# RWKV attention and two MLPs on one core: k transposes and y^T halves as single steps of the planner

## The chip, the cores and the metric

One NeuronCore of a Trainium2 chip. Its engines run side by side, each in its own program order: TensorE (PE) multiplies matrices, VectorE (DVE) and ScalarE (ACT) work element by element, GpSimd (POOL) and SyncE (SP) issue DMA transfers here. The metric is the device time of one execution in microseconds (us); before the change the median of three runs is 1027.59 us (1027.45 to 1028.16).

## The reference

An RWKV-like recurrence over 4 batches of 8 heads, 768 tokens and 48 dimensions per head, then a gated MLP (384 to 1536 to 384) and a second MLP with a leaky ReLU (384 to 2048 to 384) on 3072 tokens, all in float32:

```python
for t in range(S):
    kt, vt, rt, wt = (k[:, :, t], v[:, :, t], r[:, :, t], w[:, :, t])
    cur = np.einsum('bhd,bhe->bhde', u[None] * kt, vt)
    y[:, :, t] = np.einsum('bhd,bhde->bhe', rt, state + cur)
    state = wt[:, :, :, None] * state + np.einsum('bhd,bhe->bhde', kt, vt)
...
x = y.transpose(0, 2, 1, 3).reshape(B * S, H * D)
x = (x @ moe_w_a * (x @ moe_w_b)) @ moe_w_out
h = x @ moe2_w_in
out = (np.maximum(h, 0) + alpha * np.minimum(h, 0)) @ moe2_w_out
```

## The kernel before

**Units.** The recurrence is cut into 12 units: one unit is a chunk of 128 tokens of half of the (batch, head) pairs, so units 0 and 1 are the first chunk, 2 and 3 the second, and so on. A unit holds r, k and w transposed in tile T (112 partitions: two heads of 48 with a gap; 8 pairs; 128 tokens), and again in natural layout (128 tokens on the partitions) in tile N; v is in V. Its steps are:

- *natural* (DVE, lines 440 to 503): the C x C blocks on the diagonal of the chunk (C is 4 or 8 in units 0 to 3, 16 from unit 4 on), diagonal by diagonal: products for the decay (kn, N), a product into e and a reduction into A, of 16, 15, 14, ... columns a block. *diag* (SP, lines 505 to 522) sends A to DRAM (mb) and back into M with eight transfers.
- *tree* (DVE, lines 525 to 543): six steps h = 1, 2, 4, ... 32 on T, each a large one (1024 elements a partition) on r and k and a small one on w. *level* (PE, psl, lines 545 to 594): for each h from C on, the off-diagonal blocks of M by small matmuls from T, copied to M by ACT; level h needs the tree steps below h, so unit 3 (C = 8) begins with h = 8, behind the step h = 4.
- *ktrans* (lines 605 to 621): eight transposes of k on PE (psk), copied to kn by ACT in two groups of four.
- *dstate* (psd, lines 623 to 646): the chunk's contribution to the state; *state* (lines 651 to 693): copies of the state St to Z (ACT), its decay, and DVE's St += psd.
- *yout* (psx, lines 695 to 730): y^T from M and Z, two halves b of 64 matmuls each; each half goes to x as a rounded part (ACT) and a rest (DVE).

**MLP1** runs between the units on PE. A block j of 512 tokens (two units) takes 12 steps f: pa (nine matmuls, since float32 is split in two parts and three products of three matmuls are added), pb (nine), and acc for the step before (six, then three). Between them ACT copies pa to a, DVE multiplies a by pb (the product, `a<-a,pb`), ACT rounds it to g and DVE takes the rest (`g<-a,g`). Lines 257 (helper `tt`) and 769 (helper `mm`) show most of these instructions. Each block's MLP1 lies beside the next block's two units. Weights come in through POOL's DMAs and are unpacked by ACT and DVE (ws, w). **MLP2** (hp, acd) follows from about 613 us on, when all units are done.

**What sets the order.** `Tasks` (lines 35 to 208) is a list planner. Each step is added with an engine, a planned duration, a priority, the names that it reads and writes, and a pool from which it takes a buffer (`alloc`). `run` plays the plan forward: on each engine that is free it starts the ready step of lowest priority number, and emits the instructions in the order of planned starts. The hardware then keeps this order on every engine. A planned duration is thus no time on the chip, but it decides what the planner puts ahead of what. Pool psatt has three PSUM banks, given out in program order to psl, psk, psd, psx; psh has two (pa, pb, hp), so a pb takes the bank that the pb before it had, once DVE's product has read it; T, N, V, kn and e have one buffer each, so the next unit's T is loaded only when the tree, the levels and the transposes of this unit are done with T.

An empty PE step (duration 0, no instruction) can take a bank for a step that needs two; *dstate* did so already.

The calls of a unit that the change touches, priorities by `pr`:

```python
        for g in range(2):
            ktrans(g, pr(0.6))
        dstate(pr(0.65))
        ...
        yout(0, pr(0.8))
        yout(1, pr(0.85))
```

Of the kernel before, what the change touches and what calls it, by code (L numbers as in the profile page):

```python
# [7 lines left out]
F32 = mybir.dt.float32  # L8
# [26 lines left out]
class Tasks:  # L35
# [26 lines left out]
    def add(self, eng, dur, prio, fn, r=(), w=(), alloc=None, nbytes=0, work=0):  # L62


        i = len(self.t)
        deps = set()
        for x in r:
            if x in self.last_w:
                deps.add(self.last_w[x])
        for x in w:  # L70
            if x in self.last_w:
                deps.add(self.last_w[x])
            deps.update(self.readers.get(x, ()))
        for x in r:
            self.readers.setdefault(x, []).append(i)
        for x in w:
            self.last_w[x] = i
            self.readers[x] = []
        if alloc:
            tag, name = alloc  # L80
            self.handles[name] = (tag, [], i)
            self.pool_seq[tag].append(i)
        for x in list(r) + list(w):
            h = x.split("/")[0] if isinstance(x, str) else x
            if h in self.handles:
                self.handles[h][1].append(i)
                if self.handles[h][2] != i:
                    deps.add(self.handles[h][2])
        self.t.append([eng, dur, prio, fn, deps, alloc, nbytes])
        if work:  # L90
            self.work[i] = work
        return i
# [119 lines left out]
def rwkv_then_moe_kernel(  # L212
# [49 lines left out]
    def act(n, psum=False):  # L262
        return n / 1200 + (0.05 if psum else 0.093)
# [70 lines left out]
    X = {}  # L334

    def unit(u, pr):
# [265 lines left out]
            else:  # L602
                nc.scalar.copy(dst, src)

        def ktrans(g, p):
            st = {}
            ps = f"psk{u}_{g}"
            tag, pool = bank(False)

            def tr():  # L610
                st[g] = pp.tile([128, 4, 112], F32, tag=tag, name="psk", bufs=3)
                for i in range(4):
                    nc.tensor.transpose(st[g][:, i], cur["T", u][:, 1, 4 * g + i], idt[0:112, 0:112])

            def cp():
                if g == 0:
                    cur["kn", u] = new_kn().rearrange("p (q d) -> p q d", d=112)
                nc.scalar.copy(cur["kn", u][:, 4 * g:4 * g + 4], st[g])

            add("PE", 0.4, p, tr, r=[f"{T}/k.{g}", "idt"], w=[ps], alloc=(pool, ps), work=392)  # L620
            add("ACT", act(448, True), p, cp, r=[ps], w=[f"{kn}/{g}"], alloc=("kn", kn) if g == 0 else None)

        def dstate(p):

# [67 lines left out]

                add("ACT", act(384, True), p + 6, begin, r=[f"psd{u}_{cc}"], w=s)

        def yout(b, p):


            st = {}
            ps = f"psx{u}_{b}"
            t0 = 256 * (u - us[0]) + 128 * b  # L700
            tag, pool = bank(False)

            def mms():
                st["ps"] = pp.tile([128, 3, 128], F32, tag=tag, name="psx", bufs=3)
                for cc in range(2):
                    for q in range(4):
                        for s, c0, hd, beg, end in (
                                (2 * q, 0, 0, True, True), (2 * q + 1, 32, 1, True, True),
                                (8 + q, 32, 0, True, False), (8 + q, 0, 1, False, True)):
                            nc.tensor.matmul(  # L710
                                out=st["ps"][32 * (s % 4):32 * (s % 4) + 32, s // 4, 64 * cc:64 * cc + 64],
                                lhsT=zt(cc, hd)[:, 4 * b + q, c0:c0 + 32],
                                rhs=mt(hd)[:, cc, 4 * b + q],
                                start=beg, stop=end,
                            )

            def hi():
                if first:
                    X[j] = xp.tile([128, 2, 3, 256 * len(us)], F32R, tag="x", name="x", bufs=2)
                nc.scalar.copy(X[j][:, 0, :, t0:t0 + 128], st["ps"])  # L720

            def lo():
                tt(X[j][:, 1, :, t0:t0 + 128], st["ps"], X[j][:, 0, :, t0:t0 + 128].bitcast(F32), ALU.subtract)

            first = u == us[0] and b == 0
            add("PE", 1.56, p, mms, w=[ps], alloc=(pool, ps), work=2048,
                r=[mn(hd, k) for hd in range(2) for k in KM]
                + [zn(cc, hd, k) for cc in range(2) for hd in range(2) for k in "VS"])
            add("ACT", act(384, True), p, hi, r=[ps], w=[f"x{j}/{u}{b}h"], alloc=("x", f"x{j}") if first else None)
            add("DVE", dve(384), p, lo, r=[ps, f"x{j}/{u}{b}h"], w=[f"x{j}/{u}{b}l"])  # L730


        if u:
# [18 lines left out]
        for bs in parts_:  # L752
            for hd, b0 in ((0, 64), (1, 0)):
                e, d = ("DVE", dve(512 * len(bs), True)) if both and hd else ("ACT", act(512 * len(bs)))
                add(e, d, p, lambda hd=hd, b0=b0, bs=bs: rcopy(hd, b0, bs), r=nm(T + "/r", bs), w=[mn(hd, "R")])
        for g in range(2):
            ktrans(g, pr(0.6))
        dstate(pr(0.65))
        for cc in range(2):
            for bs in parts_:  # L760
                state(cc, bs, pr(0.7 + 0.05 * cc))
        yout(0, pr(0.8))
        yout(1, pr(0.85))

        return [f"x{j}/{u}{b}{z}" for b in range(2) for z in "hl"]

# [379 lines left out]
```

## Time and profile before

| | |
|---|---|
| median of 3 runs | 1027.59 us (1027.45 to 1028.16) |
| profiled execution | 1034.63 us, span 1032.8 us |
| mean granted PE clock | 0.986 |
| PE busy | 988.8 us (96%) |
| DVE busy | 728.4 us (71%) |
| ACT busy | 434.1 us (42%) |
| POOL busy | 95.7 us (9%) |
| chain that ended last | PE 65%, DVE 12%, ACT 10%, DMA 9%, issue 3%, SPq 1% |

Read the table by stretches. Up to some 83 us the first units run almost alone; from there to 541 us units and MLP1 share PE; from 613 us on it is MLP2. In a timeline row, the first number is the start, the second the duration, then come the engine, the line, the operation and the tiles (out <- in), shapes and the count of instructions in the row; in brackets the idle time of the engine before it and what ended it. Durations overlap the next start a little, since engines are pipelined.

### The profile page before, as it was taken

To read this page: it belongs to the slowest core of one execution; us is meant where nothing else is said; L and a number is where in the kernel's file an instruction comes from. 1 tells how busy PE (TensorE), PEld (TensorE's weight loads), DVE (VectorE), ACT (ScalarE), POOL (GpSimd) and SP (SyncE) were. 2 spreads that over 40 slices of the span, in tenths; PEclk is the share of its full clock that TensorE was granted. 3 is DMA by queue.
4 is the path that set the end of the run, shared out by engine and by line. 5 is a ranking of instruction groups with operands and counts; after the bars stand their busy time and mean duration, and the time that the engine had idled before them with its cause. 6 is when DMAs were issued, how large, how long until landed. Compare 5 with 4: busy or idle time off the path is not lost.

```text
span 1032.8 us, 22660 instructions
## 1 busy us (share of the span) xinstructions
PE 988.8 (96%) x9616; PEld 850.3 (82%) x9616; DVE 728.4 (71%) x1215; ACT 434.1 (42%) x930; POOL 95.7 (9%) x173
## 2 busy tenths in 40 slices
PE   6869889999999999999999999999999999999998
PEld 5768767778788888878888887989998999999988
DVE  7868897989899898797944667455554554555544
ACT  2475989354353553534347995121221211221111
POOL 3032350100000010001003431000000000000000
PEclk9898999999999999999999999999999999999999
DMA  9483585051441424325115552010010100000000
GB/s 278 107 233 110 143 248 137 33 138 36 130 133 21 125 69 120 88 55 169 20 42 168 169 183 78 1 31 31 1 55 7 31 31 1 1 31 1 31 1 31
DMA packets 75092, 85.70 MB, mean 83 GB/s; under 512 B 55216, under 2 KB 64560, under 8 KB 72368
## 3 DMA queue, kind: packets, MB, share of 16 engines
q1 hardware_dynamic: 67824, 52.81, 19.2%
q0 software_dynamic: 7168, 31.46, 9.5%
q8 instruction: 75, 1.23, 0.5%
q14 instruction: 25, 0.20, 0.1%
HBM read 73.24 MB, written 11.01 MB: 82 GB/s over the span
## 4 chain that ended last, share of the span: by engine, by line
PE 65%; DVE 12%; ACT 10%; DMA 9%; issue 3%; SPq 1%; POOL 0%; ACTq 0%; DVEq 0%; POOLq 0%
PE acd L769 19%; PE hp L769 19%; PE acc L769 7%; PE pa L769 6%; PE pb L769 6%; DVE T L257 3%; DMA T<-in_rkw_t_dram 3%; DVE e L257 2%; PE psl L567 2%; DVE A L486 2%; PE warm L988 2%; ACT ws L301 2%; DMA n<-in_rkw_n_dram 2%; ACT ws L295 2%; PE psx L710 2%
## 5 line engine op out<-in xcount | busy, mean ns | idle before, releaser
L769 PE MATMUL acd<-w,g 128*128 128x384 f32 x1152 | 216.9, 336 | 0.2 <-ACT x L855 0.2
L769 PE MATMUL hp<-x,w 128*128 128x512 f32 x864 | 214.9, 393 | 1.5 <-DVE g L927 1.5
L769 PEld LDWEIGHTS acd<-w,g 128*128 128x128 f32 x1152 | 203.8, 188 | 8.6 <-ACT x L855 0.5
L932 ACT CAST g<-g 128x512 fp32r<-128x512 f32 x96 | 59.8, 623 | 304.1 <-PE acd L769 262.1
L769 PEld LDWEIGHTS hp<-x,w 128*128 128x128 f32 x864 | 161.1, 188 | 31.5 <-DVE g L927 1.9
L769 PE MATMUL acc<-g,w 128*128 128x512 f32 x648 | 173.9, 396 | 0.0
L257 DVE TENSOR_TENSOR g<-g,g 128x512 fp32r<-128x512 f32 x96 | 66.2, 690 | 150.6 <-ACT g L932 150.6
L769 PE MATMUL pb<-x,w 128*128 128x512 f32 x648 | 161.2, 393 | 1.7 <-issue 1.7
L769 PE MATMUL pa<-x,w 128*128 128x512 f32 x648 | 160.7, 392 | 0.0
L769 PEld LDWEIGHTS pb<-x,w 128*128 128x128 f32 x648 | 121.4, 189 | 27.7 <-issue 2.1
L769 PEld LDWEIGHTS pa<-x,w 128*128 128x128 f32 x648 | 120.7, 188 | 26.5 <-ACT w L316 0.5
L769 PEld LDWEIGHTS acc<-g,w 128*128 128x128 f32 x648 | 118.5, 188 | 24.1
L257 DVE TENSOR_TENSOR T<-T 112x1024 f32<-112x1024 f32 (+3 forms) x144 | 116.5, 811 | 21.2 <-DMA T<-in_rkw_t_dram 17.2
L831 ACT CAST g<-a 128x512 fp32r<-128x512 f32 x72 | 44.6, 620 | 132.6 <-DVE a L257 130.0
L923 DVE TENSOR_SCALAR g<-hp,al 128x512 f32<-128x512 f32 x96 | 72.1, 751 | 25.5 <-PE hp L769 23.0
L486 DVE TENSOR_REDUCE A<-e 128x16 f32<-128x768 f32 (+15 forms) x148 | 86.1, 582 | 1.7
L257 DVE TENSOR_TENSOR a<-a,pb 128x512 f32<-128x512 f32 x72 | 49.2, 683 | 28.1 <-PE pb L769 25.7
L927 DVE SCALAR_TENSOR_TENSOR g<-hp,g 128x512 f32<-128x512 f32 x96 | 66.3, 691 | 3.0
L820 ACT COPY a<-pa 128x512 f32<-128x512 f32 x72 | 42.1, 584 | 36.2 <-PE pa L769 35.8
L257 DVE TENSOR_TENSOR g<-a,g 128x512 fp32r<-128x512 f32 x72 | 49.6, 689 | 10.0 <-ACT g L831 10.0
L567 PEld LDWEIGHTS psl<-T 48*16 48x16 f32 (+3 forms) x3072 | 34.3, 99 | 25.8 <-issue 12.2
L567 PE MATMUL psl<-T 48*16 48x16 f32 (+3 forms) x3072 | 38.0, 183 | 15.2 <-DVE T L257 8.4
(68 smaller groups left out, 900.0 us busy)
## 6 DMA issues: line engine op xcount, KB each, us to landing
raw<-in_wt_dram POOLq DMA_DIRECT2D x68, 384.0 KB, 4.1
T<-in_rkw_t_dram SPq DMA_DIRECT2D x12, 1344.0 KB, 9.0
N<-in_rkw_n_dram SPq DMA_DIRECT2D x10, 1152.0 KB, 8.4
x2d<-x POOLq DMA_DIRECT2D x36, 128.0 KB, 2.1
x2r<-x2d SPq DMA_DIRECT2D x36, 128.0 KB, 2.3
out_dram<-o SPq DMA_DIRECT2D x24, 192.0 KB, 1.9
V<-in_v_s_dram SPq DMA_DIRECT2D x11, 384.0 KB, 8.5
Z<-in_v_s_dram SPq DMA_DIRECT2D x44, 96.0 KB, 3.1
```

What stands on the lines that cost most here:

```text
L257: nc.vector.tensor_tensor(out=out, in0=a, in1=b, op=op)
L295: nc.scalar.activation(out=c["s"].bitcast(F16).rearrange("p (n b) -> p n b", b=2)[:, :, 1], in_=c["raw"][:, :, 1].bitcast(F32), func=ACTF. ...
L301: nc.scalar.activation(out=c["s"].bitcast(U16).rearrange("p (n b) -> p n b", b=2)[:, :, 0], in_=c["raw"][:, :, 0], func=ACTF.Copy, scale=7 ...
L486: nc.vector.tensor_reduce(out=v[:, :, d:d + (n - 1) * (SUB + 1) + 1:SUB + 1], in_=part(st["e"], 0, n), axis=AX.X, op=ALU.add)
L567: nc.tensor.matmul(out=st["ps"][o0:o0 + ms, cc, q, zc * i:zc * i + zc], lhsT=t[b0:b0 + 48, 1, q0 + q, t0:t0 + ms], rhs=r[b0:b0 + 48, q0 + ...
L710: nc.tensor.matmul(out=st["ps"][32 * (s % 4):32 * (s % 4) + 32, s // 4, 64 * cc:64 * cc + 64], lhsT=zt(cc, hd)[:, 4 * b + q, c0:c0 + 32], ...
L769: nc.tensor.matmul(out=out, lhsT=lhsT, rhs=rhs, start=start, stop=stop)
L820: nc.scalar.copy(c["a", f], c["pa"])
L831: nc.scalar.copy(c["g", f][:, 0], c["a", f])
L923: nc.vector.tensor_scalar(out=st["m", f], in0=st["h", f], scalar1=0.0, scalar2=al[:, f:f + 1], op0=ALU.min, op1=ALU.mult)
L927: nc.vector.scalar_tensor_tensor(out=st["m", f], in0=st["h", f], scalar=0.0, in1=st["m", f], op0=ALU.max, op1=ALU.add)
L932: nc.scalar.copy(st["g", f][:, 0], st["m", f])
```

## The change

`ktrans` becomes one step on PE with all eight transposes and a planned duration of 0.8 (before two of 0.4). It needs both halves of k in T, and two banks at once, the first taken by an empty step. ACT's two copies follow as before. `yout` becomes, for units 2 to 11, one step with both halves and two banks, of planned duration 2 * 2.72 = 5.44 (before two of 1.56 each); for units 0 and 1 it stays two steps, the second at p + 0.05. All copies of x stand at the priority of the first half now. No instruction of a unit is added or taken away (of the fillers named warm, that keep PE busy early, there is one fewer ahead of the first pa); what changes is when the planner places them.

```diff
-        def ktrans(g, p):
+        def ktrans(p):
...
-            add("PE", 0.4, p, tr, r=[f"{T}/k.{g}", "idt"], w=[ps], alloc=(pool, ps), work=392)
-            add("ACT", act(448, True), p, cp, r=[ps], w=[f"{kn}/{g}"], alloc=("kn", kn) if g == 0 else None)
+            add("PE", 0.0, p, lambda: None, w=[f"psk{u}_0"], alloc=(pool, f"psk{u}_0"))
+            add("PE", 0.8, p, tr, r=[f"{T}/k.0", f"{T}/k.1", "idt"], w=[f"psk{u}_0", f"psk{u}_1"],
+                alloc=(pool, f"psk{u}_1"), work=784)
+            for g in range(2):
+                add("ACT", act(448, True), p, lambda g=g: cp(g), r=[f"psk{u}_{g}"], w=[f"{kn}/{g}"],
+                    alloc=("kn", kn) if g == 0 else None)
...
-            add("PE", 1.56, p, mms, w=[ps], alloc=(pool, ps), work=2048,
-                r=[mn(hd, k) for hd in range(2) for k in KM]
-                + [zn(cc, hd, k) for cc in range(2) for hd in range(2) for k in "VS"])
-            add("ACT", act(384, True), p, hi, r=[ps], w=[f"x{j}/{u}{b}h"], alloc=("x", f"x{j}") if first else None)
-            add("DVE", dve(384), p, lo, r=[ps, f"x{j}/{u}{b}h"], w=[f"x{j}/{u}{b}l"])
...
+            if u > 1:
+                add("PE", 0.0, p, lambda: None, w=[f"psx{u}_0"], alloc=(pool, f"psx{u}_0"))
+                add("PE", 2 * 2.72, p, lambda: [mms(0), mms(1)], w=[f"psx{u}_0", f"psx{u}_1"], alloc=(pool, f"psx{u}_1"),
+                    work=4096, r=r)
+            for b in range(2):
+                t0 = 256 * (u - us[0]) + 128 * b
+                ps = f"psx{u}_{b}"
+                if u < 2:
+                    add("PE", 1.56, p + 0.05 * b, lambda b=b: mms(b), w=[ps], alloc=(pool, ps), work=2048, r=r)
+                add("ACT", act(384, True), p, lambda b=b, t0=t0: hi(b, t0), r=[ps], w=[f"x{j}/{u}{b}h"],
+                    alloc=("x", f"x{j}") if u == us[0] and b == 0 else None)
+                add("DVE", dve(384), p, lambda b=b, t0=t0: lo(b, t0), r=[ps, f"x{j}/{u}{b}h"], w=[f"x{j}/{u}{b}l"])
...
-        for g in range(2):
-            ktrans(g, pr(0.6))
+        ktrans(pr(0.6))
...
-        yout(0, pr(0.8))
-        yout(1, pr(0.85))
+        yout(pr(0.8))
```

How this moves instructions is seen at three places. The first is DVE behind the seventh product of MLP1's first block, beside unit 3: its tree steps on T up to the large one of h = 4 (`112x2x128x4`), which the first psl of unit 3 needs, and the unpacking of weights (ws, w). Before:

```order
L257 TENSOR_TENSOR a<-a,pb 128x512
L257 TENSOR_TENSOR T<-T 112x256
L310 SCALAR_TENSOR_TENSOR ws<-raw,ws 128x384
L257 TENSOR_TENSOR T<-T 112x2x128x4
L257 TENSOR_TENSOR g_2039<-a,g_2039 128x512
L257 TENSOR_TENSOR T<-T 112x128
```

And after:

```order
L257 TENSOR_TENSOR a<-a,pb 128x512
L257 TENSOR_TENSOR T<-T 112x2x512
L257 TENSOR_TENSOR w<-ws,w 128x384
L257 TENSOR_TENSOR T<-T 112x512
L310 SCALAR_TENSOR_TENSOR ws<-raw,ws 128x384
L257 TENSOR_TENSOR T<-T 112x2x256x2
L257 TENSOR_TENSOR w<-ws,w 128x384
L257 TENSOR_TENSOR T<-T 112x256
L310 SCALAR_TENSOR_TENSOR ws<-raw,ws 128x384
L257 TENSOR_TENSOR T<-T 112x2x128x4
L257 TENSOR_TENSOR g_2036<-a,g_2036 128x512
```

The step that psl needs was fourth in the row, counted from the product, and is tenth now. On PE, in the same place after the change, psx of unit 2 has come ahead of the three acc, the pa and that psl:

```order
L713 MATMUL psx<-M,Z 32x64 x64
L778 MATMUL acc_1404<-g_1696,w 128x512
L778 MATMUL acc_1405<-g_1696,w 128x512
L778 MATMUL acc_1406<-g_1696,w 128x512
L778 MATMUL pa<-x,w 128x512 x9
L567 MATMUL psl<-T 24x16 x64
```

The second place is DVE in a steady unit, around the psx of unit 7 (units 6 to 10 are alike). Before, from one product to the next, psx's two copies to x with natural's steps (kn, N, e, A) and the tree's:

```order
L257 TENSOR_TENSOR a<-a,pb 128x512
L257 TENSOR_TENSOR e<-kn,N 128x672
L257 TENSOR_TENSOR T<-T 112x2x128x4
L257 TENSOR_TENSOR g_5908<-a,g_5908 128x512
L257 TENSOR_TENSOR x<-psx,x 128x3x128
L486 TENSOR_REDUCE A_82<-e 128x14
L257 TENSOR_TENSOR N<-N 128x624
L257 TENSOR_TENSOR x<-psx,x 128x3x128
L257 TENSOR_TENSOR e<-N 128x624
L257 TENSOR_TENSOR T<-T 112x128
L486 TENSOR_REDUCE A_82<-e 128x13
L257 TENSOR_TENSOR T<-T 112x2x64x8
```

After, the first twelve rows from the product on:

```order
L257 TENSOR_TENSOR a<-a,pb 128x512
L257 TENSOR_TENSOR g_5774<-a,g_5774 128x512
L257 TENSOR_TENSOR kn<-N 128x672
L257 TENSOR_TENSOR St_79<-St_79,psd_5739 112x384
L257 TENSOR_TENSOR N<-N 128x672
L257 TENSOR_TENSOR e<-kn,N 128x672
L257 TENSOR_TENSOR T<-T 112x2x512
L486 TENSOR_REDUCE A_82<-e 128x14
L257 TENSOR_TENSOR St_79<-St_79,psd_5740 112x384
L257 TENSOR_TENSOR N<-N 128x624
L257 TENSOR_TENSOR T<-T 112x512
L257 TENSOR_TENSOR e<-N 128x624
```

Six more follow before the next product: two large and one small step of the tree, A of 13, e of 576 and a copy of psx to x. So both St additions, three large tree steps and psx's copy stand between the same two products now.

The third place is SP, one unit from 7 on, with the loads of the next unit (T, N, V, Z) and the round trip of A through mb to M:

```order
-L380 DMA T<-in_rkw_t_dram 112x3072
 L388 DMA N<-in_rkw_n_dram 128x2304
 L511 DMA mb_83<-A_82 128x256
+L518 DMA M<-mb_83 16x16x16 x8
+L380 DMA T<-in_rkw_t_dram 112x3072
 L398 DMA V<-in_v_s_dram 128x768
-L518 DMA M<-mb_83 16x16x16 x8
 L403 DMA Z<-in_v_s_dram 64x8x48 x4
```

T has moved from the head of the row to behind the eight transfers to M, which wait for mb.

## Rows read from the trace of the kernel before

**Rows 1.** Windows: busy us (x instructions) by engine, clock, DMA share, GB/s.

```profile
83.00:541.00 458.00, 443.44 (x5815) 361.56 (x5815) 398.66 (x698) 238.62 (x542) 42.55 (x67) 1.00 0.37 101
```

**Rows 2.** Waits of PE, 83 to 541: us in total, times, longest.

```profile
PE psl L567 <- DVE T L257: 3.9, 5, 1.0
...
PE psx L710 <- DMA M<-mb: 1.5, 2, 1.2
PE psd L637 <- ACT kn L618: 1.1, 3, 0.5
PE psk L613 <- DVE T L257: 1.0, 1, 1.0
```

**Rows 3.** Timeline of PE at psk of units 4 and 7: start, duration.

```profile
209.20 0.93 PE L613 MATMUL psk<-idt,T 112*128 112x112 f32 x8
209.90 1.64 PE L769 MATMUL acc<-g,w 128*128 128x512 f32 x6
...
338.90 0.55 PE L613 MATMUL psk<-idt,T 112*128 112x112 f32 x4
339.22 0.94 PE L769 MATMUL acc<-g,w 128*128 128x512 f32 x3
```

**Rows 4.** Timeline of PE, 432 to 452, around psd and psx.

```profile
432.11 1.14 PE L637 MATMUL psd<-V,kn 64*48 64x48 f32 x64 [0.45 <-ACT kn L618]
...
439.44 2.20 PE L769 MATMUL pb<-x,w 128*128 128x512 f32 x9
...
442.84 2.20 PE L769 MATMUL pa<-x,w 128*128 128x512 f32 x9
...
445.56 2.22 PE L769 MATMUL pb<-x,w 128*128 128x512 f32 x9
...
449.07 2.70 PE L710 MATMUL psx<-M,Z 128*32 128x64 f32 x128
```

**Rows 5.** Timeline of DVE, 440 to 456, the same stretch.

```profile
440.11 0.55 DVE L257 TENSOR_TENSOR St<-St,psd 112x384 f32<-112x384 f32 x1
...
444.68 0.68 DVE L257 TENSOR_TENSOR a<-a,pb 128x512 f32<-128x512 f32 x1
...
449.19 0.65 DVE L257 TENSOR_TENSOR T<-T 112x256 f32<-112x256 f32 x1
...
451.15 0.85 DVE L257 TENSOR_TENSOR e<-kn,N 128x672 f32<-128x672 f32 x1
451.92 1.22 DVE L257 TENSOR_TENSOR T<-T 112x1024 f32<-112x1024 f32 x1
...
454.89 0.79 DVE L257 TENSOR_TENSOR N<-N 128x624 f32<-128x624 f32 x1
```

**Rows 6.** Timeline of DVE and PE at unit 3's first level.

```profile
142.14 1.23 DVE L257 TENSOR_TENSOR T<-T 112x1024 f32<-112x1024 f32 x1
...
143.47 1.42 PE L567 MATMUL psl<-T 48*24 48x16 f32 x128 [0.56 <-issue]
```

**Rows 7.** Timeline of SP's queue and DVE, units 4 and 7.

```profile
210.91 0.38 SPq L511 DMA_DIRECT2D mb<-A  x1
...
216.32 7.71 SPq L518 DMA_DIRECT2D M<-mb  x8
...
340.62 0.33 SPq L380 DMA_DIRECT2D T<-in_rkw_t_dram  x1
...
343.18 0.39 SPq L511 DMA_DIRECT2D mb<-A  x1
...
348.21 1.23 DVE L257 TENSOR_TENSOR T<-T 112x1024 f32<-112x1024 f32 x1 [1.44 <-DMA T<-in_rkw_t_dram]
...
351.18 4.53 SPq L518 DMA_DIRECT2D M<-mb  x8
```

**Rows 8.** Windows of two early stretches, columns as in rows 1.

```profile
66.00:72.00 6.00, 2.69 (x70) 2.36 (x70) 4.16 (x11) 4.70 (x11) 0.71 (x2) 1.00 1.00 235
...
76.00:82.00 6.00, 4.24 (x46) 4.07 (x46) 2.29 (x5) 2.68 (x6) 1.71 (x3) 0.51 0.74 186
```

More of the change, by code (lines that the diff above doesn't have):

```diff
@@ L603, in rcopy, with cp @@
                 nc.scalar.copy(dst, src)
-        def ktrans(g, p):
+        def ktrans(p):
             st = {}
-            ps = f"psk{u}_{g}"
             tag, pool = bank(False)
             def tr():
[L611 to L615, printed above, removed]
+                for g in range(2):
+                    st[g] = pp.tile([128, 4, 112], F32, tag=tag, name="psk", bufs=3)
+                    for i in range(4):
+                        nc.tensor.transpose(st[g][:, i], cur["T", u][:, 1, 4 * g + i], idt[0:112, 0:112])
+            def cp(g):
                 if g == 0:
@@ L618, in cp @@
                 nc.scalar.copy(cur["kn", u][:, 4 * g:4 * g + 4], st[g])
-            add("PE", 0.4, p, tr, r=[f"{T}/k.{g}", "idt"], w=[ps], alloc=(pool, ps), work=392)
-            add("ACT", act(448, True), p, cp, r=[ps], w=[f"{kn}/{g}"], alloc=("kn", kn) if g == 0 else None)
+            add("PE", 0.0, p, lambda: None, w=[f"psk{u}_0"], alloc=(pool, f"psk{u}_0"))
+            add("PE", 0.8, p, tr, r=[f"{T}/k.0", f"{T}/k.1", "idt"], w=[f"psk{u}_0", f"psk{u}_1"],
+                alloc=(pool, f"psk{u}_1"), work=784)
+            for g in range(2):
+                add("ACT", act(448, True), p, lambda g=g: cp(g), r=[f"psk{u}_{g}"], w=[f"{kn}/{g}"],
+                    alloc=("kn", kn) if g == 0 else None)
         def dstate(p):
@@ L693, in state, with yout, mms @@
                 add("ACT", act(384, True), p + 6, begin, r=[f"psd{u}_{cc}"], w=s)
-        def yout(b, p):
+        def yout(p):
             st = {}
-            ps = f"psx{u}_{b}"
-            t0 = 256 * (u - us[0]) + 128 * b
             tag, pool = bank(False)
-            def mms():
-                st["ps"] = pp.tile([128, 3, 128], F32, tag=tag, name="psx", bufs=3)
+            def mms(b):
+                st[b] = pp.tile([128, 3, 128], F32, tag=tag, name="psx", bufs=3)
                 for cc in range(2):
@@ L710, in mms @@
                             nc.tensor.matmul(
-                                out=st["ps"][32 * (s % 4):32 * (s % 4) + 32, s // 4, 64 * cc:64 * cc + 64],
+                                out=st[b][32 * (s % 4):32 * (s % 4) + 32, s // 4, 64 * cc:64 * cc + 64],
                                 lhsT=zt(cc, hd)[:, 4 * b + q, c0:c0 + 32],
@@ L715, in mms, with hi, lo @@
                             )
-            def hi():
-                if first:
+            def hi(b, t0):
+                if u == us[0] and b == 0:
                     X[j] = xp.tile([128, 2, 3, 256 * len(us)], F32R, tag="x", name="x", bufs=2)
[L720 to L725, printed above, removed]
-            add("PE", 1.56, p, mms, w=[ps], alloc=(pool, ps), work=2048,
-                r=[mn(hd, k) for hd in range(2) for k in KM]
-                + [zn(cc, hd, k) for cc in range(2) for hd in range(2) for k in "VS"])
-            add("ACT", act(384, True), p, hi, r=[ps], w=[f"x{j}/{u}{b}h"], alloc=("x", f"x{j}") if first else None)
-            add("DVE", dve(384), p, lo, r=[ps, f"x{j}/{u}{b}h"], w=[f"x{j}/{u}{b}l"])
+                nc.scalar.copy(X[j][:, 0, :, t0:t0 + 128], st[b])
+            def lo(b, t0):
+                tt(X[j][:, 1, :, t0:t0 + 128], st[b], X[j][:, 0, :, t0:t0 + 128].bitcast(F32), ALU.subtract)
+            r = ([mn(hd, k) for hd in range(2) for k in KM]
+                 + [zn(cc, hd, k) for cc in range(2) for hd in range(2) for k in "VS"])
+            if u > 1:
[10 more added lines that the diff above has]
+                add("DVE", dve(384), p, lambda b=b, t0=t0: lo(b, t0), r=[ps, f"x{j}/{u}{b}h"], w=[f"x{j}/{u}{b}l"])
         if u:
```

## The prediction

> **What bounds the kernel now.** I read the busy table by stretches first, then PE's waits in the stretch that the change touches, then PE's, DVE's and SP's own rows at the places where the order moves. From 83 to 541 us attention units and MLP1 share PE: it is busy 443.44 of 458 us [rows 1]. So PE sets the end, and there are two ways to move it: less time between PE's starts, or a change in the 14.6 us (458 - 443.44) that it waits. The waits with one cause each are small: first levels psl behind the tree steps on T 3.9 us in five places, psx behind the arrival of M 1.5, psd behind the copies to kn 1.1, psk of unit 2 behind T 1.0 [rows 2]. DVE is the second engine: 398.66 of 458 us busy [rows 1], and its buffers come back just in time. The prelude and MLP2 keep their order, so nothing is counted there.
>
> **The merged steps themselves: nothing.** Two psk steps of four transposes take PE from start to start 339.22 - 338.90 = 0.32 us each, so 0.64; one step of eight in unit 4 took 209.90 - 209.20 = 0.70 us [rows 3]. Seven units change from 4+4 to 8, between -0.2 and +0.5 us in all. The halves of psx bring nothing either: in the kernel before, both halves already stand next to each other in all twelve units, one run of 128 matmuls [rows 4]. I add up the starts of all PE work from the first pa to the end of MLP1 in the order of either kernel, and take **-0.2 us**. So the change acts by what it moves. The planner now believes that psx is one step of 5.44 us (it took 2.70 [rows 4]), wants both banks at once, and places it some 9.5 us earlier in units 6 to 10, 4 to 12 in units 4 and 5; psk and psd come 2 to 3 us later. DVE's and SP's orders follow.
>
> **Waits that go.** Unit 4's psx waited for M; in the new order its M is issued earlier against PE: -1.5 [rows 2]. psd no longer comes right behind the kn copies in units 9 and 11: -0.9 of the 1.1. Three of the five waits of psl for the tree (1.0, 1.0, 0.3 of the 3.9) go, since these levels come later on PE than their tree step: -2.4. Sum -4.8. In unit 2 psk comes after its T step and the two behind it with it: -1.0 [rows 2], and -0.3 at its psd and psx.
>
> **Unit 3's first level: +2.7.** Before, the tree step that it needs starts 142.14 and lasts 1.23 us, and the psl follows at 143.47 after 0.56 us idle [rows 6] (named "issue"; the step's end, 143.37, is 0.10 us ahead, so it is that step). Now this step is not fourth behind the product a on DVE but tenth. A row's duration overlaps the next row's start by some 0.08 us (451.92 - 451.15 = 0.77 for 0.85), so start to start it needs: a 0.6, three T steps of 1024 elements 1.14 each (1.22), two small ones 0.6 and 0.55 (0.65 for 256 elements), and four weight steps of 384 elements at 0.47, like St (0.55) [rows 5]: 7.1 us. PE in between has psx, 2.63 (2.70 less the overlap), and three acc and a pa, 2.72 (445.56 - 442.84) [rows 4], 5.35 us. So PE waits at least 7.1 + 0.1 - 5.35 = 1.9 us. If DVE starts its product late, the wait grows by as much: the product of 444.68 starts 3.0 us behind the end of its pb (439.44 + 2.20 = 441.64) [rows 4, 5], one that finds DVE idle starts at once. I take the middle, 1.4, so 3.3 of 1.9 to 4.9, less the 0.56 of before. One later level, the 32-row psl of unit 4, comes 6 us earlier on PE and waits some +0.9 (0 to 1.5) for its tree step.
>
> **DVE in one stretch per unit: +4.2.** This is the term on which the sign hangs. Between two products a, DVE must do what the order puts there, and the pb after next needs the bank that the product reads. In the stretch around psx of a steady unit the new order has 18 DVE instructions: a and g 0.6 each, two St and one x 0.47 each, three large T 3.4, two small T 1.2, and eight of natural between 0.67 and 0.77 (e 0.77, N 0.71), 5.9: 13.1 us [rows 5], and 0.7 us more where g stands right behind its a and has to wait for ACT's copy. PE needs 1.07 for psd (1.14 less the overlap), 6.12 for one round of pb, acc, pa (445.56 - 439.44) and 2.63 for psx: 9.8 us [rows 4]. In the kernel before the stretch around psx holds 12 instructions, about 9 us by the same durations. The bank gives DVE a slack: the pb that began 439.44 ended 441.64, its product ended 445.36 (444.68 + 0.68), and the next pb began 445.56, 0.20 us later [rows 4, 5], so a product that starts more than 3.2 us behind its pb stops PE. Starting with no lag, DVE falls behind by 13.1 + 0.7 - 9.8 = 4.0 us, 0.8 over the slack: I take 0.75 us each in units 7, 8 and 9, 1.05 in unit 6 (13.45 us of DVE work by the same durations). In unit 3, 12.2 us of DVE stand against 8.95 of PE, 0.85 more. Units 4, 5 and 10 (11.2 against 8.95, 12.07 against 9.8) end inside the slack. Sum 1.05 + 2.25 + 0.85 = 4.15. Bounds: 0, if DVE starts the stretch with all its work done ahead (by the same durations its other stretches are lighter now, 2 to 5.5 us instead of 5.4 to 7.5), and 6.2, if it starts half a product late.
>
> **SP: +2.2.** From unit 6 on, the T of the next unit is issued behind the eight M transfers, which wait for mb. Before, T was issued 340.62 and its first tree step ran 348.21, 7.6 us later; mb was issued behind it at 343.18 and M at 351.18, 8.0 us later. Where T was not ahead, M followed mb by 5.4 us (210.91 to 216.32) [rows 7]. So M comes 2.6 us sooner (psx of unit 5, which now comes early, still waits: +0.7), and T is issued about 5.4 + 4.5 (the eight issues take 4.53) = 9.9 us behind mb and starts its tree 7.6 later, 17.5 us behind mb. mb itself is earlier against PE, because DVE's natural now ends well ahead of psk; against DVE's turn for T this leaves 0 to 0.9 us per unit. I take 1.5 us for five units, of 0 to 4.5.
>
> **Sum.** -0.2 - 4.8 - 1.3 + 2.7 + 0.9 + 4.2 + 0.7 + 1.5 = **+3.7 us**. The profiled execution took 1034.63 us (span 1032.8), 7.0 us above the median of three runs, 1027.59; I lay the difference on the median: **1031.3 us**.
>
> **The clock.** In 76 to 82 us PE was busy 4.24 of 6 us and granted 0.51, the level of 1.2 GHz; in 66 to 72 it was busy only 2.69 us and kept 1.00, 2.4 GHz [rows 8]. So a wait of this length may cost a slow stretch or none. The Trainium skill, page "TensorE: Matmul & The Clock Gate", section "What's actually happening", says that the low clock is the default, that it returns when PE idles, and that activity lifts it: by it, the new wait of unit 3 would bring the clock down, which the 76 to 82 row bears out and the 66 to 72 row does not. It is rival 4.
>
> **Rivals.**
> 1. *No difference.* DVE starts every crowded stretch with nothing left over and the 4.2 us fall to nothing: 1031.3 - 4.2 = 1027.1. For it: the other stretches got lighter by as much. Against it: the sum of 13.1 against 9.8 starts from almost no lag already. Here also belongs that the change does nothing by what it says: the halves were adjacent before.
> 2. *Faster.* Besides, T is in time (-1.5), unit 3 waits only 1.9 (-1.4), and the level of unit 4 finds its step done (-0.9): 1023.3. It decides from the point at which DVE's lag at a product stays under 3.2 us in units 3 and 6 to 9. For it: psx is consumed earlier, so the waits of psl and psd that went stay away.
> 3. *Slower by SP.* T's transfer ends after DVE's turn for it, and DVE stands, with the products queued behind it: 4.5 instead of 1.5, and the lag past the slack rises by as much in three of the five units, some 1.5: 1035.8. It decides from 17.5 us between mb and the tree's turn.
> 4. *Slower by the clock.* PE falls to 0.51 behind the wait of unit 3. At half speed a 6 us window as that of rows 8 loses up to 2.9 us: 1034.
>
> **How the numbers follow.** Chances: forecast 0.40, no difference 0.21, faster 0.27, SP 0.07, clock 0.05. A measurement of this kernel can tell about 0.2% (2.1 us) from no change. Of the forecast's case some 0.05 lies within that, of the rivals 1 and 2 some 0.04 crosses from the one to faster and 0.02 back: faster 0.29, same 0.24, slower 0.47. The range takes rival 2 and rival 3 in with some 0.7 us to spare at the low end, and DVE's upper bound (+2) on the SP case at the high end: 1022.6 to 1038. Forecast 1031.3.
>
> **What would show it.** In the profile after: psx some 9 us earlier in units 6 to 10; a wait of PE at pb behind DVE's product in units 6 to 9, which the kernel before has nowhere (right), or products that start under 3.2 us behind their pb (rival 1 or 2); one wait of 2 to 5 us at the first level of unit 3; DVE's waits for T in units 7 to 11 above 0.9 us (rival 3); a granted clock of 0.5 behind 141 us (rival 4). PE's busy time from 83 us to MLP1's end should not move by more than 0.5 us; if it does, the merge was worth something, and my first step is wrong.

## The result, and the profile after

The changed kernel takes 1042.59 us (median of five runs, 1039.55 to 1044.31) against 1028.16 us for the kernel before (five runs): 1.3% slower, ratio 1.013 with a 95% interval of 1.0114 to 1.0146. The forecast of 1031.3 us had the sign and missed the size; the time lies above its range, which ended at 1038. Single executions of three kernels below and one of the kernel before took 1215 us and more; the medians and ratios below leave them out.

The two profiled executions, 1039.55 us after and 1034.63 us before, differ by less than the medians. That one of before had lost 6 us ahead of the first pb (85.17 us, after 79.11), where psx waited 4.78 us with "issue" as the releaser. So I compare from the start of the first pb to that of the 60th, a stretch with 5,824 matmuls between its ends in both. Windows, columns as in rows 1, first of the kernel before, then of the one after:

```profile
85.17:545.68 460.51, 445.95 (x5825) 363.64 (x5824) 398.53 (x698) 240.18 (x544) 42.55 (x67) 1.00 0.36 99
```

```profile
79.11:550.77 471.66, 450.39 (x5825) 364.54 (x5824) 402.74 (x702) 240.72 (x547) 38.63 (x70) 0.99 0.37 99
```

The same work takes 11.15 us more. PE waits 21.27 us instead of 14.56 (+6.7), and is *busy* 4.4 us longer with the same instructions. PE's waits of after in that stretch, beside those of rows 2 (us in total, times, longest):

```profile
PE psl L567 <- issue: 5.8, 2, 3.4
PE pb L778 <- DVE a L257: 5.8, 5, 2.4
PE psx L713 <- ACT Z L668: 2.1, 4, 1.1
PE pa L778 <- ACT a L829: 2.0, 2, 1.7
PE psd L642 <- ACT kn L619: 1.8, 3, 1.4
PE psl L567 <- DVE T L257: 1.4, 1, 1.4
PE psl L567 <- ACT M L585: 0.9, 1, 0.9
PE psx L713 <- DMA M<-mb: 0.6, 1, 0.6
```

The second line is new: pb waits for DVE's product, which the kernel before had nowhere. So is most of the first line, two stops of 3.36 us (unit 3's first level) and 2.46 us (a level of unit 7, shown at the end), and the fourth. Below are DVE's and PE's timelines where it is largest, beside unit 9; they answer to rows 4 and 5.

```profile
437.12 0.69 DVE L257 TENSOR_TENSOR a<-a,pb 128x512 f32<-128x512 f32 x1 [1.23 <-PE pb L778]
438.50 0.69 DVE L257 TENSOR_TENSOR g<-a,g 128x512 fp32r<-128x512 f32 x1 [0.69 <-ACT g L840]
...
441.11 0.86 DVE L257 TENSOR_TENSOR e<-kn,N 128x672 f32<-128x672 f32 x1
444.05 1.23 DVE L257 TENSOR_TENSOR T<-T 112x1024 f32<-112x1024 f32 x1 [2.09 <-DMA T<-in_rkw_t_dram]
...
451.50 1.22 DVE L257 TENSOR_TENSOR T<-T 112x1024 f32<-112x1024 f32 x1
452.63 0.55 DVE L257 TENSOR_TENSOR x<-psx,x 128x384 fp32r<-128x384 f32 x1
453.10 0.68 DVE L257 TENSOR_TENSOR a<-a,pb 128x512 f32<-128x512 f32 x1
```

```profile
442.32 2.70 PE L713 MATMUL psx<-M,Z 128*32 128x64 f32 x128
444.96 2.35 PE L778 MATMUL pb<-x,w 128*128 128x512 f32 x9
...
450.55 0.84 PE L778 MATMUL acc<-g,w 128*128 128x512 f32 x3
453.83 2.64 PE L778 MATMUL pb<-x,w 128*128 128x512 f32 x6 [2.44 <-DVE a L257]
```

From product to product DVE needs 453.10 - 437.12 = 15.98 us: the 13.1 of the forecast, 0.69 for g behind ACT, and 2.09 for T, which had not landed. PE has 9.8 us of work there, and stands still. Its clock does not stay up behind the stop; windows of unit 3's first level and of that place (the clock column is a share of 2.4 GHz; its low level is 0.50, 1.2 GHz):

```profile
134.00:142.00 8.00, 5.42 (x141) 4.68 (x142) 8.00 (x16) 7.57 (x16) 3.65 (x5) 0.79 1.02 189
454.00:458.00 4.00, 4.00 (x11) 3.12 (x12) 4.00 (x7) 0.92 (x2) 0.00 (x0) 0.57 0.01 4
```

### The profile page after: what moved, and what is told of

Its sections match the earlier page's. It is cut to its first block, busy times and chain, and to the rows that moved or that the text cites. A ratio compares the mean times of both kernels' runs of the same rounds, so it can differ in the third digit from the quotient of the medians.

```text
span 1037.8 us, 22635 instructions
## 1 busy us (share of the span) xinstructions
PE 990.5 (95%) x9612; PEld 848.6 (82%) x9612; DVE 730.4 (70%) x1215; ACT 432.4 (42%) x930; POOL 88.8 (9%) x173
## 4 chain that ended last, share of the span: by engine, by line
PE 62%; DVE 16%; ACT 12%; DMA 5%; issue 4%; SPq 0%; POOL 0%; ACTq 0%; DVEq 0%; POOLq 0%
PE acd L778 19%; PE hp L778 19%; PE pb L778 6%; PE pa L778 6%; PE acc L778 6%; DVE T L257 4%; DMA T<-in_rkw_t_dram 3%; DVE e L257 3%; DVE A L486 3%; PE warm L997 2%; ACT ws L301 2%; ACT ws L295 2%; PE psl L567 2%; ACT raw L307 2%; ACT w L316 2%
## 5 line engine op out<-in xcount | busy, mean ns | idle before, releaser
L567 PEld LDWEIGHTS psl<-T 48*16 48x16 f32 (+3 forms) x3072 | 34.2, 100 | 25.5 <-issue 14.4
L310 DVE SCALAR_TENSOR_TENSOR ws<-raw,ws 128x384 uint32<-128x384 uint32 x68 | 37.6, 556 | 18.3 <-ACT ws L301 18.1
```

Of the source, the lines that this page charges most:

```text
L310: nc.vector.scalar_tensor_tensor(out=c["s"], in0=c["raw"][:, :, 1], scalar=3, in1=c["s"], op0=ALU.logical_shift_left, op1=ALU.bitwise_or)
L567: nc.tensor.matmul(out=st["ps"][o0:o0 + ms, cc, q, zc * i:zc * i + zc], lhsT=t[b0:b0 + 48, 1, q0 + q, t0:t0 + ms], rhs=r[b0:b0 + 48, q0 + ...
```

## The experiments

**Which part of the change it is.** Theory A: the loss comes from the place that the planner gives psx, since it now believes 5.44 us for it (3.12 before), and from what DVE's order becomes. Rival B: merged steps that take two banks at once, and the later psk, hold things up. Four kernels tell them apart. The kernel before with the merged k transposes only (the `ktrans` part of the diff):

> The kernel before with only the k transposes merged into one step. Theory A (the loss comes from where psx goes, since the planner believes 5.44 us for it, and from what DVE then has to do between two products): psx and SP's T keep their places of before here, no crowded stretch on DVE beside units 6 to 10, so within 3 us of the kernel before (1025 to 1031) and no wait of pb for the product above 0.5 us in all. Theory B (the steps that take two banks at once, and the later psk, hold things up): 5 us or more slower, above 1033, with T's transfers awaited longer.

Measured: 1029.5 us, ratio 1.003 (1.0008 to 1.0051); no wait of pb for the product. The kernel before with the merged `yout` only:

> The kernel before with only the y^T halves merged (planned 5.44 us). Theory A: psx comes early in units 5 to 10, T goes behind M on SP, DVE has 11.0 to 11.9 us between two products around psx against 8.9 of PE (13.4 to 13.8 against 10.1 in the changed kernel), so about half of its loss: +4 to +9 us over the kernel before, pb waits for the product 1 to 3 us in all. Theory B: slower as well, since two banks are taken at once, +5 or more.

Measured: 1039.11 us, ratio 1.0108 (1.0093 to 1.0123); pb waits 3.9 us for the product in five places. Both are above what theory A allowed (4 to 9 us, 1 to 3 us of waits): the loss is 10 us here. Both merges, with another planned time:

```diff
-                add("PE", 2 * 2.72, p, lambda: [mms(0), mms(1)], w=[f"psx{u}_0", f"psx{u}_1"], alloc=(pool, f"psx{u}_1"),
+                add("PE", 2 * 1.32, p, lambda: [mms(0), mms(1)], w=[f"psx{u}_0", f"psx{u}_1"], alloc=(pool, f"psx{u}_1"),
```

> The changed kernel, both merges kept, but the planner told 2.64 us for the y^T step instead of 5.44 (psx of both halves took 2.70 before). Theory A: psx, T on SP and DVE's stretches go back to about their places of before, so within 4 us of the kernel before (1024 to 1032), and 10 us or more faster than the changed kernel. Theory B: nothing that it blames is changed, so 1037 or more.

Measured: 1026.58 us, ratio 0.9986 (0.9965 to 1.0006). And the kernel before with nothing merged:

```diff
-            add("PE", 1.56, p, mms, w=[ps], alloc=(pool, ps), work=2048,
+            add("PE", 1.56 if u < 2 else 2.72, p, mms, w=[ps], alloc=(pool, ps), work=2048,
```

> The kernel before, nothing merged, but the planner told 2.72 us for each half of y^T of units 2 to 11 instead of 1.56. Theory A: the order becomes nearly that of the y^T merge alone, so the same time as that kernel within 3 us: +4 to +9 us over the kernel before, without any merged step. Theory B: no merge, so no loss: within 2 us of the kernel before.

Measured: 1037.84 us, ratio 1.0095 (1.0075 to 1.0115). PE's waits in it:

```profile
PE pb L769 <- DVE a L257: 3.5, 3, 2.0
PE psl L567 <- DVE T L257: 3.3, 3, 1.7
PE psl L567 <- issue: 3.0, 1, 3.0
PE psx L710 <- DMA M<-mb: 1.6, 3, 1.2
```

The number alone, without any merged step, costs about as much as the merge with it (0.95% and 1.08%), and the merges without the number cost nothing. B falls. The same once more, with what the kernel before planned for both halves (`2 * 1.56`):

> The changed kernel, both merges kept, with 2 * 1.56 = 3.12 us planned for the y^T step, which is what the kernel before planned for its two halves together. Theory A: no crowded stretch (the order is that of the k merge alone), so 1025 to 1032, within 3 us of the kernel before. Theory B (merged steps cost): 1034 or more.

Measured: 1028.5 us, ratio 1.0008 (0.9984 to 1.0032).

**Whether DVE's amount of work is the cause.** The natural steps were cut to 16 of 48 columns, the planned durations left, so the order of the instructions on every engine is the same and only DVE has less to do:

```diff
-                return x.rearrange("p (g j) d -> p g j d", j=C)[:, :, lo:lo + m]
+                return x.rearrange("p (g j) d -> p g j d", j=C)[:, :, lo:lo + m, 0:DW]
...
+            DW = 16 if u > 5 else D
```

> The kernel before, with the diagonal products and reductions of units 6 to 11 on 16 of their 48 columns (the rest of their values is left out), so that DVE has about 18 us less per unit there, with the planned durations and so the order unchanged. It is the base for the same cut of the changed kernel. DVE's lag at a product is at most 3.0 us in the kernel before and stops PE nowhere, so both theories expect little: 1024 to 1030.

> The changed kernel with the same cut (units 6 to 11 on 16 of 48 columns, the rest left out), its order unchanged. Theory A (DVE has too much between two products): beside units 6 to 11 the waits of pb for the product, 4.4 us there, and the slow clock behind the longest one vanish; what is left against the same cut of the kernel before is the part beside units 2 to 5, by the traces about 5 us. So +4 to +7 us over it. Theory C (psx early waits for something else, or SP's late T holds the tree): the cut does not touch that, +10 to +14 us remain.

Measured: 1023.94 us (ratio 0.9976, 0.9954 to 0.9998) and 1031.97 us (1.0044, 1.0024 to 1.0064); the difference of the medians falls from 14.4 us to 8.0, and that of the ratios from 1.3% to 0.7%. This lies between the ranges of the two theories (4 to 7 and 10 to 14 us), so the times alone do not decide; the traces do for this stretch. Windows from the 25th pb to the 60th, beside the units whose work was cut, 3,096 matmuls from end to end in all four. Before, after, before with the cut, after with the cut:

```profile
285.54:545.68 260.14, 257.85 (x3097) 211.53 (x3096) 222.64 (x394) 114.01 (x257) 8.57 (x17) 1.00 0.31 84
```

```profile
280.50:550.77 270.27, 261.75 (x3097) 212.27 (x3096) 218.38 (x383) 113.44 (x257) 10.86 (x23) 0.99 0.32 83
```

```profile
278.23:535.87 257.64, 257.64 (x3097) 211.55 (x3096) 160.52 (x390) 115.58 (x257) 8.33 (x17) 1.00 0.31 85
```

```profile
282.98:543.59 260.61, 258.27 (x3097) 211.56 (x3096) 155.69 (x369) 114.98 (x257) 10.86 (x23) 1.00 0.33 86
```

The gap in this stretch shrinks from 10.1 us (270.27 - 260.14) to 3.0 (260.61 - 257.64), and PE's busy time falls from 261.75 to 258.27 us: with the waits goes the slow clock. Of the 4.3 us of pb's waits there 0.7 us remain, although DVE waits longer than before for T's landing there (6.8 us in four places, the longest 3.9; before the cut 2.6 in two, the longest 2.1). So beside units 6 to 11 these waits come from DVE's amount of work between two products, and T's lateness alone does not make them. It is not the whole gap: the stop of 2.46 us in unit 7, which waits for nothing in the profile, is gone with the cut as well, and why is not shown. pa keeps its 1.7 us behind ACT's copies.

**Early or late.** The long planned time in units 2 to 5 only, and in units 6 to 11 only (`2 * (2.72 if u < 6 else 1.32)` and the reverse):

> The changed kernel with 5.44 us planned for the y^T step of units 2 to 5 only, 2.64 for the others. By the traces, the changed kernel lost 5.4 us up to the end of MLP1's second block against the one with 2.64 everywhere, most of it at unit 3's first level (3.4 us wait) and its psx. Theory A: 1031 to 1035, with that wait of 2 to 4 us. A theory by which only the steady units lose expects 1028.

> The changed kernel with 5.44 us planned for the y^T step of units 6 to 11 only, 2.64 for the others. Three stretches on DVE are crowded (13.5 us against 10.1 of PE, 11.9 against 8.9, 12.2 against 9.5) instead of five in the changed kernel. Theory A: waits of pb for the product 1 to 3 us in all, none at unit 3's first level above 1.5; 1030 to 1035. A theory by which the loss is all early expects 1028.

Measured: 1035.63 us, ratio 1.0071 (1.0043 to 1.0099), a little above what theory A allowed, and 1033.83 us, ratio 1.0066 (1.0043 to 1.009). Both halves lose about the same. But in the trace of the second, pb waits for the product less than theory A expected (1 to 3 us), unit 3's first level holds a stop of 3.0 us that theory A did not expect, and psx waits 3.4 us for M, in the changed kernel 0.6. PE's waits from the first pb to the 60th:

```profile
PE psl L567 <- issue: 4.6, 2, 3.0
PE psx L713 <- DMA M<-mb: 3.4, 3, 2.6
...
PE pb L778 <- DVE a L257: 0.9, 1, 0.9
```

So the planned time of the late units costs by itself, but in that kernel most of the waits are others than those for the product.

**What the early half is.** My forecast had put most of it on unit 3's first level. Taking the long time from unit 2 alone (`2 * (1.32 if u == 2 else 2.72)`) should have shown it:

> The changed kernel with 2.64 us planned for the y^T step of unit 2 alone, 5.44 for the others. Unit 2's psx then no longer comes between unit 3's tree steps and its first level. Theory A: the wait of 3.4 us at that level falls under 1.5 us, and with it the slow clock of some 2 us behind it goes; 4 to 6 us faster than the changed kernel, 1036 to 1039. If the early loss lies elsewhere, the wait moves and 1041 to 1043 remain.

Measured: 1042.65 us (two runs), nothing gained: a miss. The wait for the tree went, but PE stopped in the same psl all the same, and psx of unit 5 waited 3.6 us for M, since the planner had shifted all that follows. PE's rows of that kernel:

```profile
140.43 1.21 PE L567 MATMUL psl<-T 48*24 48x16 f32 x126 [0.86 <-PE acc L778]
144.61 0.22 PE L567 MATMUL psl<-T 48*24 48x16 f32 x2 [2.97 <-issue]
...
267.58 0.27 PE L713 MATMUL psx<-M,Z 128*32 128x64 f32 x2 [3.62 <-DMA M<-mb]
```

Four more runs asked what remained: the cut of DVE's work from unit 2 on (`u > 1` in the diff above), and the long time in unit 2 alone and in unit 3 alone.

> The kernel before with the diagonal products and reductions of units 2 to 11 on 16 of their 48 columns (the other columns' part is left out), the order unchanged: the base for the next run. It lost little to DVE in the later units (3.9 us less by the same cut there), and its early waits are for T, M and Z: 1017 to 1024.

> The changed kernel with the same cut in units 2 to 11 (the other columns' part is left out), its order unchanged. Theory A for the early part (DVE has too much between two products there as well): what was left of the difference after the cut in units 6 to 11, 8.1 us, falls to 3 us or less. Theory D (early, the order makes PE wait for M, kn, Z and the instructions themselves, not for DVE's amount of work): 5 us or more remain.

Measured: 1018.21 us (five runs, 1013.92 to 1020.67; ratio 0.9913, 0.9878 to 0.9947) and 1025.09 us (ten runs, 1020.04 to 1030.25; ratio 0.9983, 0.9955 to 1.0012). By the medians 6.9 us of difference remain, where theory A expected 3 or less; with these intervals it may be a few us less or more. The two traces say otherwise. Windows from the first pb to the 25th, 2,728 matmuls, before and after with this cut:

```profile
80.49:274.42 193.93, 186.32 (x2729) 151.30 (x2728) 139.12 (x309) 126.37 (x287) 32.77 (x50) 1.00 0.43 124
78.77:273.37 194.60, 187.48 (x2729) 153.11 (x2728) 145.26 (x332) 127.90 (x291) 24.56 (x47) 0.98 0.43 123
```

The early part differs by 0.7 us (194.60 - 193.93); with the cut in units 6 to 11 only, it differed by 4.3 (201.59 against 197.32). From the first pb to the 60th 3.5 us remain (454.88 against 451.42), 1.9 of them longer busy time. So the traces speak for DVE's work in the early half too, and the times do not; the traced execution of the base was its slowest of five. How much of the early loss is DVE's amount of work stays open.

> The changed kernel with 5.44 us planned for the y^T step of unit 2 alone, 2.64 for the others: psx of unit 2 comes between unit 3's tree steps and its first level, everything later is near the order with 2.64. If the wait of PE there costs its 3.4 us, 3 to 5 us over the kernel with 2.64 everywhere (1027.6), so 1030 to 1033. If another stop of 2.8 us, in which PE waits for nothing the profile shows, lies at the same level there anyway and only changes place with it, 1026 to 1029.

> The changed kernel with 5.44 us planned for the y^T step of unit 3 alone, 2.64 for the others. One stretch beside it is heavier on DVE (11.3 us against 8.9 of PE, inside the slack of 3.2), nothing else is moved far: 1025 to 1030, no loss above 2 us.

Measured: 1024.74 us, ratio 0.9975 (0.9956 to 0.9994), below both ranges and nearer to the one for a stop that changes place. Its traced execution was its slowest of eleven (1031.91 us, with the first pb only at 85.58), but from the first pb to the 60th it takes 457.6 us with a wait of 3.6 us at unit 3's first level, and the kernel with 2.64 everywhere 457.1 with a stop of 2.8 us inside that level. So the wait takes the place of a stop that is there without it, and costs next to nothing more. And 1029.15 us, ratio 1.0038 (1.0014 to 1.0062), inside the range, but 4 us over the former, against my 2 us: unit 3's own early psx does cost. The rows of this last kernel on PE, from the eleventh pb on:

```profile
184.61 2.33 PE L778 MATMUL pb<-x,w 128*128 128x512 f32 x9 [1.53 <-DVE a L257]
186.78 2.20 PE L778 MATMUL acc<-g,w 128*128 128x512 f32 x9
190.79 1.21 PE L567 MATMUL psl<-T 48*16 48x16 f32 x128 [1.81 <-issue]
```

The pb waits for a product that DVE brings late, and the next level for the tree step behind it (named "issue"; that step ends at 190.69 us, 0.10 ahead). The changed kernel has the same pair (1.44 and 1.36 us, at 177.50 and 192.79).

**Whether SP's order matters.** T of units 7 to 11 from POOL's queue instead of SP's, so that it no longer stands behind M:

```diff
-            nc.sync.dma_start(out=cur["T", u][:, :, q0:q1], in_=rkw_t[u, :, :, q0:q1])
+            (nc.gpsimd if u > 6 else nc.sync).dma_start(out=cur["T", u][:, :, q0:q1], in_=rkw_t[u, :, :, q0:q1])
...
-            add("SP", 0.6, p0, lambda bs=bs: ld_t(bs), r=after_diag,
+            add("Pool" if u > 6 else "SP", 0.6, p0, lambda bs=bs: ld_t(bs), r=after_diag,
```

> The changed kernel with T of units 7 to 11 loaded from POOL's queue, so that it no longer stands behind M on SP; DVE's crowded stretches stay. If SP's late T is a part of the loss, DVE's waits for T (3.4 us, the longest 2.1 in unit 10's) go and the longest wait of pb for the product falls from 2.4 to about 0.9: 2 to 4 us faster, 1038 to 1041. If the order on DVE alone decides, the waits of pb stay above 5 us in all.

Measured: 1049.07 us (two runs), 6 us slower than the changed kernel: a miss. T was hardly issued earlier. In the changed kernel, unit 7's psk and the SP queue behind it (rows 7 have the same place of before):

```profile
336.72 3.76 SPq L518 DMA_DIRECT2D M<-mb  x8
...
343.67 0.33 SPq L380 DMA_DIRECT2D T<-in_rkw_t_dram  x1
```

```profile
342.66 0.93 PE L614 MATMUL psk<-idt,T 112*128 112x112 f32 x8
```

M's issues end at 340.5, 3.2 us before T's; psk ends at 343.6. T, here that of unit 8, waited for its buffer, and POOL's queue issued it at 344.11 us for the same reason. Units 10 and 11 are alike: their T goes out some 0.1 us behind the end of psk. The T of units 7 and 9 did stand behind M, 2.2 and 1.1 us past the end of psk (294.63 and 388.89 us, T at 296.82 and 389.99), but DVE did not wait there. The run is no clean test of the queue: the planner, told of POOL, also placed DVE's steps anew beside units 7, 9 and 11, with the first tree step further ahead, and DVE now waits 1.30, 2.53 and 1.09 us for T there. How far this makes the kernel slower still (DVE waits 9.4 us for N and 8.8 for T, against 5.9 and 3.4) was not settled.

**A version that beats both.** The planner told what PE was seen to need, for psx and for psd:

```diff
-            add("PE", (1.03 if apart else 1.2) * nd, p, run, r=[kn + "/0", kn + "/1", V], w=[f"psd{u}_{i}" for i in range(nd)],
+            add("PE", 0.55 * nd, p, run, r=[kn + "/0", kn + "/1", V], w=[f"psd{u}_{i}" for i in range(nd)],
...
-                add("PE", 2 * 2.72, p, lambda: [mms(0), mms(1)], w=[f"psx{u}_0", f"psx{u}_1"], alloc=(pool, f"psx{u}_1"),
+                add("PE", 2 * 1.32, p, lambda: [mms(0), mms(1)], w=[f"psx{u}_0", f"psx{u}_1"], alloc=(pool, f"psx{u}_1"),
```

> The changed kernel with the durations that PE was seen to need: 2.64 us planned for the y^T step instead of 5.44, 1.1 for psd of two chunks instead of 2.4. No stretch on DVE holds over 3.1 us more than PE's. Theory A: no waits of pb for the product above 0.5 us in all, and at least as fast as the kernel before: 1022 to 1029.

Measured: 1020.89 us (1017.64 to 1025.06), ratio 0.9939 (0.9914 to 0.9963), 7 us faster than the kernel before and 22 us faster than the changed one. PE's waits in it, from the first pb to the 60th, the longest five:

```profile
PE pa L778 <- issue: 2.9, 1, 2.9
PE acc L778 <- ACT g L840: 2.4, 2, 1.6
PE psl L567 <- DVE T L257: 1.6, 4, 0.6
PE psl L567 <- issue: 1.0, 1, 1.0
PE psl L567 <- ACT M L585: 1.0, 1, 1.0
```

No pb waits for a product, and no matmul of MLP1 there runs at the slow clock. This kernel differs from that with 2.64 us alone (ratio 0.9986) in psd's number only, so what it gains beyond that comes with psd's number; psd's number without psx's was not tried.

## Why the forecast was wrong

The forecast added 3.7 us, 3.9 of it in PE's waits and -0.2 in PE's work. The medians differ by 14.4. In the traces it is 11.2: 6.7 in waits and 4.4 in PE's busy time. The step that failed by most is that a wait costs its idle time alone and leaves PE's busy time as it was; besides, a stop of 2.46 us and a wait of 2.0 were in no term. Term by term:

- *The merged steps: nothing.* Right. Without the planned time they cost between -0.14% and +0.3%, and with it the order alone costs nearly what the merge costs.
- *Unit 3's first level: +2.7.* The size of the wait came out (3.3 forecast, 3.36 measured, psl at 136.59), and DVE's ten rows took from 129.30 to 136.48, 7.18 us for 7.1. That the sum fits is in part luck: DVE began its product 3.1 us behind the end of its pb, where I took 1.4, and PE needed 7.1 us from that end to the level for my 5.35, in part since psx waited 0.8 us for Z on the way. The price was wrong. In the kernels with the same early order and no such wait, PE stops in the same psl for 2.8 to 3.0 us with nothing to wait for, which my sum did not know; the wait takes the place of that stop. The run with only this wait was not slower than the kernel before.
- *DVE in one stretch per unit: +4.2.* The mechanism is right, and its size in waits nearly: 5.8 us in five places (1.44 in unit 3, 0.71 in unit 6, 0.86, 0.30 and 2.44 in units 7 to 9). Units 7 and 8 came out at 0.86 and 0.30 for 0.75; unit 9 was worse, since T landed late on top. The pb that waits is the next one behind the pb whose product is late (453.83 us behind 444.96), not the one after next, as I had put it.
- *SP: +2.2.* The mechanism failed where it mattered. In units 7 and 9 T did stand behind M, and DVE did not wait. In unit 10, where DVE waited 2.09 us at its first tree step, T waited for its buffer, which psk gave back some 2 us of PE's work later than before. psx waited 0.6 us for M, as said (0.7).
- *Waits that go: -6.1.* Too much. The waits of psl for T fell by 2.5 us, as said, psk's 1.0 went; but psx for M fell by 0.9 only, and psd for kn rose from 1.1 to 1.8 instead of losing 0.9. Together the named waits gave 3.7 us. (The three waits that I let go add up to 2.3, not 2.4.)
- *In no term.* PE stopped 2.46 us in a level of unit 7 with nothing to wait for, and pa waited 2.0 us for ACT's copies, which it did nowhere before. Against that a stop of 1.67 us of the kernel before, in a pb at 147.69, went as well.
- *PE's busy time within 0.5 us.* I had named this as a test, and it failed: PE was busy 4.4 us longer with the same matmuls. Taking each matmul from its start to the next one's start, or to its own end where that comes first, 1.5 us of it is the slow clock (13 matmuls of MLP1 at half speed after, 5 before), some 1.0 lies in psx, psk and psd, and 0.7 at the starts and ends of runs of large matmuls, where the next one starts some 300 to 390 ns later instead of 227; there are nearly as many of these before (121) as after (122). The last 1.3 us are mostly in eleven matmuls within a run, whose next one starts 286 to 391 ns later: PE was held up there, but about as long as such a matmul's own row lasts (389 ns), and so no idle time shows. I had priced each wait by its idle time alone, and given the clock to a rival with a chance of 0.05 and one place. The Trainium skill, page "TensorE: Matmul & The Clock Gate", section "What's actually happening", has the clock fall when PE idles; 454 to 458 us (0.57, behind a stop of 2.44 us) agrees, but stops of 2.46, 1.67 and 0.86 us at 326, 290 and 361 us left it up, and one of 1.67 us in the kernel before was followed by 0.50 (147.8 to 151.2 us). So the length of a single stop did not tell here whether the clock falls.
- *From the profile to the median.* I laid the difference of two traces on a median. The changed kernel's profiled execution was its fastest of five: its mean granted clock was 0.988, that of its three slowest runs 0.982, where 19 runs of the kernel before had 0.986 to 0.993. So the medians differ by 3 us more than the traces do. The lower clock goes with it; what put it lower in those runs was not traced. The mean clock is no sure sign of the time: the fastest run of the kernel with the long time late (1031.34 us) had 0.938.

So it was the forecast case, with its central term near enough, and what was missing is what a stop costs beyond its idle time, and stops that no instruction explains. The upper bound of 1038 left that out too: it contained more waiting, but no dearer waiting. Beside units 2 to 5 the cause of the loss stays in part open: unit 3's psx costs about 4 us by itself, and times and traces disagree on how much of it goes with DVE's work.

## What to carry to other kernels

In a planner that orders instructions by planned durations, a duration is a command: before merging two steps, look at which number the merged step gets, and change the number alone once. When a step moves, add up what every in-order engine then has to do between two instructions that give a buffer back, and compare that with the bound engine's work in the same stretch; the difference less the buffer's slack is a first estimate of the wait (0.75 us here, for 0.86, 0.30 and, with a late transfer on top, 2.44). And price a stop of the matmul engine by more than its idle time.

## What the runs showed of the hardware that was not expected

PE can stop in the middle of a run of matmuls that wait for nothing in the profile, at the same instruction in several kernels. Beside the kernel with unit 2 short above, three kernels with the same early order stop 2.77 to 3.04 us two matmuls before the end of unit 3's first level, and the changed kernel stops seven before the end of a level of unit 7:

```profile
322.42 1.16 PE L567 MATMUL psl<-T 48*16 48x16 f32 x121
...
326.04 0.23 PE L567 MATMUL psl<-T 48*16 48x16 f32 x7 [2.46 <-issue]
```

The run with the long time early stops at the same seven matmuls (2.13 us), the one with it late too (1.61). It need not happen: the changed kernel with units 6 to 11 cut has the same matmuls in the same order and runs through this place without a stop, and with no wait shortly before it. In 320 to 328 us the changed kernel's instruction queue moved two packets; that PE waited for its own instructions is a reading of this, not shown. The Trainium skill, page "Runtime: NRT & Kernel Launch", section "Instruction fetch mechanics", calls the cost of crossing from one block of instructions to the next mostly hidden. No run here shows that these stops are such crossings; if they are, up to 3.0 us of one was not hidden.
